# Another order for two early steps of a fused attention and feed-forward kernel: states ahead of outputs, first rows by token blocks, a copy split over two engines

## The chip, the cores and the metric

The kernel runs on one core of one Trainium2 chip. The metric is the device time of one execution in microseconds (us). Before the change it was 206.26 us, the median of three runs (206.10 to 206.67). TensorE is the matmul engine; VectorE, ScalarE and GpSimd are the three engines for elementwise work (DVE, ACT and POOL in the profile); SyncE issues the transfers.

## The reference

A linear attention with a decay per head (4 batches, 8 heads, 768 positions, head size 64) feeds a feed-forward layer with 512 inputs, 2048 hidden units and a tanh gelu. All inputs and the output are 32-bit floats.

```python
for b in range(nb):                       # 12 blocks of 64 positions
    intra = einsum('bhic,bhjc->bhij', qb, kb) * Dmask
    intra = einsum('bhij,bhjd->bhid', intra, vb)
    inter = einsum('bhid,bhde->bhie', qb * lam_pow, kv_state)
    out[:, :, sl] = intra + inter
    kv_state = lam_block * kv_state + einsum('bhsd,bhse->bhde', kb * rev_pow, vb)
# ... (x = out as 3072 tokens of 512 numbers)
h = x @ w_in                              # 512 -> 2048
return gelu_tanh(h) @ w_out               # 2048 -> 512
```

## The kernel before

The attention is worked through in 24 steps (12 blocks of 256 positions, each for two halves of the heads). A step is: scale q, k and v (`prep`), transpose q and k on TensorE and copy them back (`stage_t`), form the scores, mask them (`causal`), form the products with v for the state and for the outputs (`products`), copy x out (`x_out`), and update the state (`update`, part "t" on VectorE, part "u" on GpSimd). Two PSUM banks, `OK`, hold the state products (columns 256 and up) and the outputs (columns 0 to 255) of one step.

The feed-forward part waits in a list of small pieces, `filler`; `fill(n)` draws the next n pieces into TensorE's program between the attention's steps. Weights arrive as 32-bit floats and are cast. Here is the stretch that the change rewrites, as code, with cuts marked. The first rows of the feed-forward part (`Hps`) need x of steps 0 and 1 for token block 0 and x of steps 2 and 3 for token block 1, and chunks c = 0, 1 or 2, 3 of w_in.

```python
def x_out(s, OK):                                   # x of one step, two banks
    ...
    for c in range(2):
        pin(nc.scalar.activation(out=dst[...], in_=OK[c][:, 0:256]..., func=AF.Copy))

# first rows of group 0: (chunks, token blocks, last)
((0, 1), both, False), ((2, 3), b0, False), ((2, 3), b1, True)
...
update(1, 0)
idle(3)                        # three products that nobody reads
scores(2); products(2, None)
causal(2); prep_v(3)
update(2, 0); update(1, 1); update(2, 1, "t")
idle(2)
stage_t(3)
OK1 = products(None, 1, evacuate=False)[0]
OK2 = products(None, 2, evacuate=False)[0]
x_out(2, OK2); x_out(1, OK1)
scores(3)
banks = products(3, None)
update(3, 0)
cast_win(0, 0, 256, 128, c01)                       # VectorE, two casts
cast_win(0, 256, 512, 256, c01, on_act=True)
causal(3); queue_group(0)
fill(4)
products(None, 3, banks)
cast_win(0, 0, 512, 256, c23)
fill(8)
...
cast_wout(1, (POOL, ACT)); cast_wout(3, (POOL, ACT))
fill(9)                                             # output sums O2, four products each
prep(4); stage_t(4)                                 # q of step 4 on VectorE, then the transposes
```

The transposes of step 4 stand in TensorE's program behind nine pieces of the output sums and need q of step 4 from VectorE. And the results of the output sums go out through three buffers, so the fourth one of group 0 needs the first to have left:

```python
o32 = otp.tile([P, DM], FP32, tag="o32", name="o32")          # otp has 3 buffers
pin(nc.scalar.activation(out=o32[:], in_=O2.pop(tau)[0][:], func=AF.Copy))
pin(nc.sync.dma_start(out=out[...], in_=o32[:]))
```

Of the kernel before, what the change touches and what calls it, by code (L numbers as in the profile page):

```python
# [10 lines left out]
AF = mybir.ActivationFunctionType  # L11
# [4 lines left out]
def kernel(  # L16
# [217 lines left out]
    def stage_t(s):  # L234
        if s >= FIRST_DMA_T:
            return
        tq, tk = a16[s][:2]
        Tps = ps_M.tile([P, 2, 2, 2, P], FP16, tag="M", name="Tps")
        for i, t in enumerate((tq, tk)):
            for hp in range(2):  # L240
                for j in range(2):
                    pin(nc.tensor.transpose(Tps[:, i, j, hp, :], t[:, j, 2 * hp : 2 * hp + 2, :],  # L242
                                            ident[:]))
        o = qkp.tile([P, 2, 2, 2, P], FP16, tag="qkT", name=f"qkT_{s}")
        if s == 2:
            pin(nc.scalar.activation(out=o[:, 0], in_=Tps[:, 0], func=AF.Copy))
            pin(nc.vector.tensor_copy(out=o[:, 1], in_=Tps[:, 1]))
        elif s in (1, 3, 5, 6):
            pin(nc.scalar.activation(out=o[:], in_=Tps[:], func=AF.Copy))
        else:  # L250
            pin(nc.vector.tensor_copy(out=o[:], in_=Tps[:]))
        qkT[s] = o
# [33 lines left out]
    def products(n, s, banks=None, evacuate=True):  # L286


        OK, opened = banks or ([ps_M.tile([P, 512], FP32, tag="M", name=f"OK{c}")
                                for c in range(2)], set())  # L290

        def start(c, hl):
            if (c, hl) in opened:
                return False
            opened.add((c, hl))
            return True

        if n is not None:
            _, tk, tv = a16[n]
            last = (n // 2) % NSB == NSB - 1  # L300
            for jk in range(2):
                for hp in range(2):
                    for c, hl in TILES:
                        if c == 1 and last:
                            continue
                        pin(nc.tensor.matmul(  # L306
                            OK[c][half64(hl), 256 + hp * D : 256 + hp * D + D],
                            tk[half64(c), jk, 2 * hp + hl, :], tv[half64(c), jk, 2 * hp + hl, :],
                            start=start(c, hl), stop=(jk == 1), skip_group_check=True))
            Kps[n] = OK  # L310
        if s is None:
            return OK, opened
        sbg, half = divmod(s, 2)
        o = qkT.pop(s)
        PT = PTs.pop(s)
        _, _, tv = a16.pop(s)
        for hp in range(2):
            for jk in range(2):
                for c, hl in TILES:
                    pin(nc.tensor.matmul(  # L320
                        OK[c][half64(hl), hp * P : hp * P + P], tv[half64(c), jk, 2 * hp + hl, :],
                        PT[half64(c), hl, hp, jk, :], start=start(c, hl), stop=False,
                        skip_group_check=True))
        for c in range(2):
            if c == 0 and sbg % NSB == 0:
                continue
            u = us.pop((s, 0) if c else (s - 2, 1))
            for hp in range(2):
                pin(nc.tensor.matmul(OK[c][:, hp * P : hp * P + P], u[:, hp].rearrange("p l d -> p (l d)"),  # L329
                                     o[:, 0, :, hp, half64(c)], start=False, stop=True,  # L330
                                     skip_group_check=True))
        if evacuate:
            x_out(s, OK)
        return OK, opened

    def x_out(s, OK):
        sbg, half = divmod(s, 2)
        g, i = group_of[sbg]
        if g not in xT:
            xT[g] = xtp.tile([P, 2, len(groups[g]), 2, SB], FP16, tag="xT", name=f"xT_{g}")  # L340
        dst = xT[g][:, half, i]
        for c in range(2):
            pin(nc.scalar.activation(  # L343
                out=dst[:, :, c * P : (c + 1) * P].rearrange("p hp (t j) -> p hp j t", j=2),
                in_=OK[c][:, 0:256].rearrange("p (hp j t) -> p hp j t", hp=2, j=2),
                func=AF.Copy))

    us = {}

    def update(s, c, parts="tu"):  # L350


        sbg, half = divmod(s, 2)
        sb = sbg % NSB
        if c == 1 and sb == NSB - 1:
            Kps.pop(s)
            return
        if "t" in parts:
            OK = Kps[s] if c == 0 else Kps.pop(s)
            K = OK[c][:, 256:384].rearrange("p (hp d) -> p hp d", hp=2)  # L360
            t = ucp.tile([P, 2, D], FP32, tag=f"t{half}", name=f"t_{s}_{c}")
            if sb == 0 and c == 0:
                pin(nc.vector.tensor_copy(out=t[:], in_=K))
            else:
                for hp in range(2):
                    pin(nc.vector.scalar_tensor_tensor(  # L366
                        t[:, hp, :], state[half][:, hp, :],
                        lamu[:, 2 * half + hp : 2 * half + hp + 1], K[:, hp, :],
                        ALU.mult, ALU.add))
            state[half] = t  # L370
        if "u" in parts:
            u = ubp.tile([P, 2, 2, D], FP16, tag=f"u{half}", name=f"u_{s}_{c}")
            pin(nc.gpsimd.tensor_tensor(  # L373
                u[:], state[half][:].unsqueeze(2).to_broadcast([P, 2, 2, D]),
                lumask[:, 2 * half : 2 * half + 2, :].unsqueeze(3).to_broadcast([P, 2, 2, D]),
                ALU.mult))
            us[(s, c)] = u
# [6 lines left out]
    def queue_group(g):  # L384
# [124 lines left out]

        def mm1_part(f, cs, blocks, last):  # L510

            if cs[0] == 0:
                first[f] = ps_M.tile([P, N], FP32, tag="M", name="Hps")
            for c in cs:
                pin(nc.tensor.matmul(by_block(first[f][:])[:, blocks],  # L515
                                     w_in16[:, c, f * P : (f + 1) * P], x(c)[:, blocks],
                                     start=(c == 0), stop=last and c == NC - 1,
                                     skip_group_check=True))
            if last:
                pin(nc.scalar.activation(out=gT[:, f % HF, f // HF, :], in_=first.pop(f)[:],  # L520
                                         func=AF.Gelu_apprx_tanh))

        if g == 0:
            both, b0, b1 = slice(0, 2), slice(0, 1), slice(1, 2)
            for fs, stages in ((range(4), (((0, 1), both, False), ((2, 3), b0, False),
                                           ((2, 3), b1, True))),
                               (range(4, 8), (((0, 1), both, False), ((2, 3), both, True)))):
                for stage in stages:
                    for f in fs:
                        filler.append(lambda f=f, stage=stage: mm1_part(f, *stage))  # L530
            for f in range(8, NF):
                filler.append(lambda f=f: mm1([f]))
            order = [(tau, part) for part in (0, 2, 1, 3) for tau in range(3)]
            order += [(3, part) for part in (0, 2, 1, 3)]
            for tau, part in order:
                filler.append(lambda tau=tau, part=part: mm2(tau, part))
            return
# [35 lines left out]
    def idle(n):  # L573

        t = ps_M.tile([P, 512], FP32, tag="M", name="idle")
        for _ in range(n):
            pin(nc.tensor.matmul(t[:], ones[:, 0:P], ones[:], start=True, stop=True))
# [40 lines left out]
    stage_t(2)  # L618
    prep_qk(3)
    update(1, 0)  # L620
    idle(3)
    scores(2)
    products(2, None)
    causal(2)
    prep_v(3)
    update(2, 0)
    update(1, 1)
    update(2, 1, "t")
    idle(2)
    stage_t(3)  # L630
    OK1 = products(None, 1, evacuate=False)[0]
    OK2 = products(None, 2, evacuate=False)[0]
    x_out(2, OK2)
    x_out(1, OK1)
    scores(3)
    banks = products(3, None)
    update(3, 0)
    c01, c23 = slice(0, 2), slice(2, 4)
    cast_win(0, 0, 256, 128, c01)
    cast_win(0, 256, 512, 256, c01, on_act=True)  # L640
    causal(3)
    queue_group(0)
    fill(4)
    products(None, 3, banks)
    cast_win(0, 0, 512, 256, c23)
    fill(8)
    cast_win(1, 0, 512, 256, c01)
    update(3, 1, "t")
    cast_win(1, 0, 512, 256, c23)
    fill(8)  # L650
    update(2, 1, "u")
# [83 lines left out]
```

## Time and profile before

| | before |
|---|---|
| time, median of 3 runs (lowest, highest) | 206.26 us (206.10, 206.67) |
| span of the profiled run | 204.3 us |
| TensorE busy | 196.8 us, 96% |
| TensorE busy from 20 to 180 us | 159.94 of 160 us |
| first feed-forward product / idle just before it | 18.08 us / 0.77 us |
| granted TensorE clock, 10 to 180 us | 1.00 |

How to read a row of a timeline: start, duration, engine, source line, operation, what is written and read, how many instructions the row joins, and in square brackets the idle time of the engine just before the row and what ended it. A row without brackets began with no idle time of note. Line numbers of the changed kernel are two or three higher than before (L401 becomes L403, L515 becomes L518, L366 becomes L368), because the change adds lines above; the copy of x, L343, becomes L348 on ScalarE and L346 on VectorE.

The kernel is bound by TensorE with no idle time from 20 us to its tail. So the only idle time to win lies ahead of 20 us, and whether a gain there reaches the end depends on whether TensorE later meets something that it doesn't set itself. The rows that show this are in the prediction.

### The profile page before, as it was taken

How to read it: one execution, taken by the hardware profiler on the slowest of the kernel's cores; microseconds unless marked ns; L12 is line 12 of the kernel's file. 1: busy time of each engine (PE TensorE's matmuls, PEld its weight loads, DVE VectorE, ACT ScalarE, POOL GpSimd, SP SyncE). 2: the span in 40 equal slices, each digit the busy share in tenths (PEclk: the TensorE clock that was granted, in tenths of full speed). 3: DMA queues.
4: the chain of work that ended last, by engine and by line, in shares of the span. 5: the costliest groups of instructions: out<-in, count | busy, mean ns of one | idle time of the engine just before them, and what ended most of it. 6: DMA issues, size and time to landing. Idle time of an engine off the chain costs nothing.

```text
span 204.3 us, 5584 instructions
## 1 busy us (share of the span) xinstructions
PE 196.8 (96%) x2321; PEld 127.6 (62%) x2321; DVE 144.8 (71%) x271; ACT 107.7 (53%) x204; POOL 70.1 (34%) x80
## 2 busy tenths in 40 slices
PE   7888999999999999999999999999999999999992
PEld 2454644456875788654688654788554788545881
DVE  4887627867599999929997828996739673136552
ACT  2364678475683573477722477641576331577110
POOL 5595123646487750436134404314412100000000
PEclk9999999999999999999999999999999999999999
DMA  4999999999999999996449993647330003300014
GB/s 132 299 321 385 387 388 379 285 291 315 297 262 228 296 241 173 235 285 176 91 128 266 181 279 94 152 107 156 75 85 0 0 3 103 107 0 0 3 51 156
DMA packets 64074, 37.86 MB, mean 185 GB/s; under 512 B 17712, under 2 KB 59184, under 8 KB 64048
## 3 DMA queue, kind: packets, MB, share of 16 engines
q1 hardware_dynamic: 63760, 37.24, 68.1%
q8 instruction: 18, 0.29, 0.6%
q10 hardware_dynamic: 288, 0.26, 0.4%
q14 instruction: 8, 0.07, 0.1%
HBM read 27.27 MB, written 6.29 MB: 164 GB/s over the span
## 4 chain that ended last, share of the span: by engine, by line
PE 89%; DMA 3%; SPq 2%; ACT 1%; DVE 1%; issue 1%
PE Hps L401 37%; PE O2ps L416 10%; PE MB L470 8%; PE MA L470 7%; PE MD L470 7%; PE Sps L271 4%; PE MC L470 4%; PE Hps L515 4%; PE OK L329 3%; PE OK L320 3%; DMA k<-in_k_dram 3%; SPq L68 2%; PE OK L306 1%; PE Tps L242 1%; DVE t L366 1%
## 5 line engine op out<-in xcount | busy, mean ns | idle before, releaser
L401 PE MATMUL Hps<-xT,w_in 128*128 128x512 f16 (+1 forms) x416 | 79.1, 346 | 0.0
L405 ACT ACTIVATE gT<-Hps 128x512 f16<-128x512 f32 x88 | 52.1, 598 | 21.9 <-PE Hps L401 21.1
L401 PEld LDWEIGHTS <-w_in 128*128 128x128 f16 x416 | 40.2, 98 | 33.5
L373 POOL TENSOR_TENSOR u<-t,lumask 128x256 f16<-128x256 f32 x40 | 31.4, 792 | 80.6 <-DVE t L366 58.4
L446 DVE TENSOR_TENSOR gs<-gT 128x512 f16<-128x512 f16 (+1 forms) x70 | 36.6, 586 | 10.8 <-ACT gT L405 10.6
L280 DVE TENSOR_TENSOR PT<-Sps,mask 128x1024 f16<-128x1024 f32 x24 | 29.2, 1216 | 17.1 <-PE Sps L271 17.1
L470 PEld LDWEIGHTS <-gs 128*128 128x128 f16 x360 | 34.9, 98 | 4.0
L211 POOL TENSOR_TENSOR v<-v,dv 128x512 f16<-128x512 f32 x24 | 29.2, 1220 | 4.9 <-DMA v<-in_v_dram 4.8
L343 ACT ACTIVATE xT<-OK 128x256 f16<-128x256 f32 x48 | 18.2, 454 | 20.0 <-PE OK L329 14.3
L416 PE MATMUL O2ps<-w_out,gT 128*128 128x512 f16 x96 | 21.9, 379 | 0.0
L226 ACT ACTIVATE qk<-k 128x512 f16<-128x512 f32 x24 | 15.0, 626 | 9.3 <-DMA k<-in_k_dram 9.3
L221 DVE TENSOR_TENSOR qk<-q,dq 128x512 f16<-128x512 f32 x23 | 19.3, 841 | 0.0
L477 ACT ACTIVATE m<-MB 128x512 f32<-128x512 f32 x9 | 5.4, 597 | 25.4 <-PE MB L470 25.4
L470 PE MATMUL MA<-w_sum,gT 128*128 128x256 f16 x144 | 17.5, 273 | 0.1
L470 PE MATMUL MD<-w_sum,gs 128*128 128x256 f16 x136 | 17.5, 273 | 0.0
L470 PE MATMUL MB<-w_out,gs 128*128 128x256 f16 x144 | 17.2, 273 | 0.0
L366 DVE SCALAR_TENSOR_TENSOR t<-t,lamu,OK 128x64 f32<-128x64 f32 x64 | 14.5, 273 | 2.3 <-PE OK L306 1.1
L470 PEld LDWEIGHTS <-gT 128*128 128x128 f16 x144 | 14.0, 98 | 2.8 <-ACT gT L405 0.3
L416 PEld LDWEIGHTS <-gT 128*128 128x128 f16 x96 | 9.2, 98 | 9.9
L481 DVE TENSOR_TENSOR o<-MA,m 128x512 f32<-128x512 f32 x9 | 6.2, 688 | 12.3 <-ACT m L477 12.3
L271 PEld LDWEIGHTS <-qkT 64*64 64x64 f16 x384 | 6.2, 106 | 8.6 <-issue 4.2
L123 DVE TENSOR_TENSOR w_sum<-wo,wo 128x1024 f16<-128x1024 f32 x6 | 7.9, 1362 | 4.2 <-DMA wo<-in_moe_w_out_dram 4.2
(55 smaller groups left out, 168.8 us busy)
## 6 DMA issues: line engine op xcount, KB each, us to landing
q<-in_q_dram SPq DMA_DIRECT2D x24, 256.0 KB, 4.5
k<-in_k_dram SPq DMA_DIRECT2D x24, 256.0 KB, 4.9
v<-in_v_dram SPq DMA_DIRECT2D x24, 256.0 KB, 4.9
out_dram<-o SPq DMA_DIRECT2D x22, 256.0 KB, 4.1
wo<-in_moe_w_out_dram SPq DMA_DIRECT2D x4, 1024.0 KB, 9.2
wi<-in_moe_w_in_dram SPq DMA_DIRECT2D x4, 512.0 KB, 8.0
wi<-in_moe_w_in_dram SPq DMA_DIRECT2D x2, 1024.0 KB, 12.5
out_dram<-o SPq DMA_DIRECT2D x2, 128.0 KB, 1.9
```

Source lines behind the costliest of these rows:

```text
L211: pin(nc.gpsimd.tensor_tensor(wide(tv[:]), ld32[s][2][:], decay(dv, s), ALU.mult))
L221: pin(q_eng.tensor_tensor(wide(tq), q32[:], decay(dq, s), ALU.mult))
L226: pin(nc.scalar.activation(out=wide(tk), in_=k32[:], func=AF.Copy))
L280: pin(nc.vector.tensor_tensor(t[:].rearrange("p a b c d -> p (a b) (c d)"), Ss.pop(n)[:].rearrange("p a b c d -> p (a b) (c d)"), mask[:]. ...
L343: pin(nc.scalar.activation(out=dst[:, :, c * P : (c + 1) * P].rearrange("p hp (t j) -> p hp j t", j=2), in_=OK[c][:, 0:256].rearrange("p ( ...
L366: pin(nc.vector.scalar_tensor_tensor(t[:, hp, :], state[half][:, hp, :], lamu[:, 2 * half + hp : 2 * half + hp + 1], K[:, hp, :], ALU.mult ...
L373: pin(nc.gpsimd.tensor_tensor(u[:], state[half][:].unsqueeze(2).to_broadcast([P, 2, 2, D]), lumask[:, 2 * half : 2 * half + 2, :].unsqueez ...
L401: pin(nc.tensor.matmul(by_block(Hps[:, i, :]), w_in16[:, c, f * P : (f + 1) * P], x(c), start=(c == 0), stop=(c == NC - 1)))
L405: pin(nc.scalar.activation(out=dst, in_=Hps[:], func=AF.Gelu_apprx_tanh))
L416: pin(nc.tensor.matmul(O2[tau][0][:], gT[:, f % HF, f // HF, tau * P : (tau + 1) * P], w_out16[:, f, :], start=(n == 0), stop=(n == NF - 1)))
L446: pin(nc.vector.tensor_tensor(gsum[m][:, i, :], block(T0, F0, i), block(T1, F1, i), op))
L470: pin(nc.tensor.matmul(dst, lhsT, rhs, start=(i == 0), stop=(i == HF - 1), skip_group_check=True))
```

## The change

The intent is to let TensorE reach its unbroken stretch earlier. The states of steps 1 and 2 go ahead of the mask of step 2; two unread products go; the transposed q and k of step 3 are copied by two engines; the first casts of w_in come ahead of the state of step 3; the first rows are drawn by token blocks, so that the first of them need neither x of step 2 nor of step 3, and four more of them stand ahead of step 3's outputs; x of step 3 is copied out by ScalarE and VectorE together. The diff, with the plain plumbing of the token blocks cut:

```diff
@@ stage_t
-        if s == 2:
+        if s in (2, 3):
             pin(nc.scalar.activation(out=o[:, 0], in_=Tps[:, 0], func=AF.Copy))
             pin(nc.vector.tensor_copy(out=o[:, 1], in_=Tps[:, 1]))
-        elif s in (1, 3, 5, 6):
+        elif s in (1, 5, 6):
             pin(nc.scalar.activation(out=o[:], in_=Tps[:], func=AF.Copy))
@@ x_out
-    def x_out(s, OK):
+    def x_out(s, OK, second=None):
...
+            if c == 1 and second is not None:
+                pin(second.tensor_copy(out=d, in_=o))
+            else:
+                pin(nc.scalar.activation(out=d, in_=o, func=AF.Copy))
@@ first rows of group 0
-            for fs, stages in ((range(4), (((0, 1), both, False), ((2, 3), b0, False),
-                                           ((2, 3), b1, True))),
+            for fs, stages in ((range(4), (((0, 1), b0, False), ((0, 1), b1, False),
+                                           ((2, 3), b0, False), ((2, 3), b1, True))),
@@ steps 2 and 3
     update(1, 0)
+    update(1, 1, "t")
     idle(3)
     scores(2)
     products(2, None)
+    update(2, 0)
     causal(2)
     prep_v(3)
-    update(2, 0)
-    update(1, 1)
+    update(1, 1, "u")
+    stage_t(3)
+    products(None, 1)
+    products(None, 2)
     update(2, 1, "t")
-    idle(2)
-    stage_t(3)
-    OK1 = products(None, 1, evacuate=False)[0]
-    OK2 = products(None, 2, evacuate=False)[0]
-    x_out(2, OK2)
-    x_out(1, OK1)
     scores(3)
     banks = products(3, None)
-    update(3, 0)
     c01, c23 = slice(0, 2), slice(2, 4)
     cast_win(0, 0, 256, 128, c01)
     cast_win(0, 256, 512, 256, c01, on_act=True)
+    update(3, 0)
     causal(3)
     queue_group(0)
-    fill(4)
-    products(None, 3, banks)
-    cast_win(0, 0, 512, 256, c23)
     fill(8)
+    cast_win(0, 0, 256, 256, c23, on_act=True)
+    cast_win(0, 256, 512, 256, c23)
+    fill(2)
+    products(None, 3, banks, evacuate=False)
+    x_out(3, banks[0], nc.vector)
+    fill(6)
+    update(3, 1, "t")
     cast_win(1, 0, 512, 256, c01)
-    update(3, 1, "t")
     cast_win(1, 0, 512, 256, c23)
     fill(8)
```

More of the change, by code (lines that the diff above doesn't have):

```diff
@@ L342, in x_out @@
         for c in range(2):
-            pin(nc.scalar.activation(
-                out=dst[:, :, c * P : (c + 1) * P].rearrange("p hp (t j) -> p hp j t", j=2),
-                in_=OK[c][:, 0:256].rearrange("p (hp j t) -> p hp j t", hp=2, j=2),
-                func=AF.Copy))
+            d = dst[:, :, c * P : (c + 1) * P].rearrange("p hp (t j) -> p hp j t", j=2)
+            o = OK[c][:, 0:256].rearrange("p (hp j t) -> p hp j t", hp=2, j=2)
+            if c == 1 and second is not None:
+                pin(second.tensor_copy(out=d, in_=o))
+            else:
+                pin(nc.scalar.activation(out=d, in_=o, func=AF.Copy))
     us = {}
@@ L510, in mm1_part @@
         def mm1_part(f, cs, blocks, last):
-            if cs[0] == 0:
+            opens = f not in first
+            if opens:
                 first[f] = ps_M.tile([P, N], FP32, tag="M", name="Hps")
@@ L516, in mm1_part @@
                                      w_in16[:, c, f * P : (f + 1) * P], x(c)[:, blocks],
-                                     start=(c == 0), stop=last and c == NC - 1,
+                                     start=opens and c == 0, stop=last and c == NC - 1,
                                      skip_group_check=True))
```

## The prediction

> **What bounds the kernel now.** I read the page first, for which engine fills the span; then the chain of waits, for what that engine waits for; then the timelines of 9 to 27 us, the only place where it waits.
>
> ```profile
> PE 196.8 (96%) x2321; PEld 127.6 (62%) x2321; DVE 144.8 (71%) x271; ACT 107.7 (53%) x204; POOL 70.1 (34%) x80
> PE   7888999999999999999999999999999999999992
> PE 89%; DMA 3%; SPq 2%; ACT 1%; DVE 1%; issue 1%
> ```
>
> TensorE is busy for 96% of 204.3 us and makes 89% of the chain. The tenths show where it is not full: the first four slices (20 us) and the tail. In the table by stretches it is busy for 3.99 of the 5 us from 15 to 20 us, and for 159.9 of the 160 us from 20 to 180 us at full granted clock. So the change, which only touches steps 2 and 3 and the first rows of the feed-forward part, can at best make TensorE reach its unbroken stretch earlier. From the timeline of TensorE:
>
> ```profile
> 13.41 0.42 PE L271 MATMUL Sps<-qkT 64*64 64x128 f16 x16 [0.50 <-DVE qkT L247]
> 15.92 0.41 PE L320 MATMUL OK<-PT,v 64*64 64x128 f16 x15 [0.17 <-DVE t L366]
> 18.08 2.11 PE L515 MATMUL Hps<-xT,w_in 128*128 128x512 f16 x8 [0.77 <-DVE w_in L107]
> ```
>
> The number in brackets is idle time before the row, with its releaser. The last row is the start of the first rows: TensorE waits 0.77 us for the first cast of w_in. VectorE's timeline says why the cast is late, and that it is slow:
>
> ```profile
> 15.02 1.23 DVE L366 SCALAR_TENSOR_TENSOR t<-t,lamu,OK 128x64 f32<-128x64 f32 x6
> 17.35 0.47 DVE L366 SCALAR_TENSOR_TENSOR t<-t,lamu,OK 128x64 f32<-128x64 f32 x2 [1.10 <-PE OK L306]
> 17.74 0.93 DVE L107 CAST w_in<-wi 128x256 f16<-128x256 f32 x2
> 17.90 1.24 POOL L373 TENSOR_TENSOR u<-t,lumask 128x256 f16<-128x256 f32 x2 [0.99 <-DVE t L366]
> ```
>
> VectorE stands idle for 1.10 us until the products of step 3 come, updates the state, and only then casts. One cast alone is 0.285 us (the shortest of its group); the two took 0.93 together, and the second ends at 18.67, just after GpSimd's first u (18.5).
>
> [...]0.93 us for two casts beside two u, and 1.52 us instead of 0.69 for the q product at 38.69 us beside a w_out cast on GpSimd. [...]the granted clock is 1.00 in all stretches[...].
>
> **The change part by part,** with the compiled order of both kernels and durations of the trace before.
>
> *States ahead of causal(2).* Both states of step 1 and 2 (four 0.19 us steps) go ahead of causal(2), which moves from 13.88 to about 14.4 and ends at 15.6. The products of step 2 then start at 15.6 instead of 15.92 (they no longer wait for the state that releases their bank): 0.3 us.
>
> *Removed unread products.* Two, 0.43 us of TensorE. The transposes behind them wait for q of step 3 (GpSimd, 14.05) anyhow: worth nothing by itself.
>
> *qkT of step 3 halved.* 0.60 on ScalarE, then 0.42 on VectorE behind causal(2): ready at about 15.95 instead of 16.0. Scores and products of step 3 come some 0.3 us earlier.
>
> *Casts ahead of the state of step 3.* The first half of w_in's first block was issued at 10.10 and landed 7.1 us later, at 17.2. So the first cast runs at 17.22 to 17.51 and TensorE starts at about 17.55 instead of 18.08: 0.5 us, and no more, since the transfer is the limit. GpSimd has no u then, so the second cast ends at 17.8 and not at 18.67.
>
> *First rows by blocks.* Eight 128x512 products (0.216 us each: 1.73) become sixteen of 128x256 (0.109: 1.75): no cost. Four of 128x256 are drawn ahead of the outputs of step 3. TensorE then does its sixteen to 19.35, four to 19.8 (the ScalarE cast of the second half, landed at 18.57, ends at 19.25), the outputs of step 3 to 20.45, where before they ended at 20.87. It is then ahead by 0.42 plus the four products (0.43): **0.85 us**.
>
> *x of step 3 on two engines.* Both outputs end by about 20.95, when TensorE has done four more products; before, ScalarE ended at 21.56. Behind it the casts of the next block are tight: GpSimd's u of step 3 lands on the second one, which may cost 0.25 us.
>
> **Where the 0.85 us goes.** TensorE has no more idle time, so an early start would come out whole if nothing else that it needs had a time of its own. But transfers do: the mean DMA share stays between 0.97 and 1.08 in every stretch from 15 to 54 us (stretches of 1 to 5 us), and no load in there waits for TensorE. I therefore looked for what is near its need already.
>
> First, transposes of step 4: TensorE begins them at 40.61; q of step 4 is ready at 38.69+1.52 = 40.21, behind the w_out casts, which follow their transfers. Ahead by 0.85, TensorE would wait until about 40.27, and keep **0.34 us**.
>
> Second, ScalarE at 53 us:
>
> ```profile
> 52.97 0.60 ACT L422 ACTIVATE o<-O2ps 128x512 f32<-128x512 f32 x1 [2.36 <-DMA out_dram<-o]
> 53.98 1.56 ACT L405 ACTIVATE gT<-Hps 128x512 f16<-128x512 f32 x3
> 54.48 0.28 PE L329 MATMUL OK<-qkT,u 128*128 128x128 f16 x2
> 54.62 1.58 PE L401 MATMUL Hps<-xT,w_in 128*128 128x256 f16 x13
> ```
>
> ScalarE stands for 2.36 us until the first output tile (issued 46.13, landing 6.7 us later) has left its buffer; there are three, and this is the fourth tile. Behind it in ScalarE's queue stand k of step 8 and the first gelu of the second group, 53.98 to 54.58. In the compiled order the Hps product at 54.62 waits for exactly this gelu, which frees its bank. TensorE came there with at most 0.02 us to spare: after the two L329 rows at 59.35 the next product follows in 0.12 us, here in 0.14. So already now this spot is set by TensorE and the output transfer at once. A TensorE that comes earlier waits there, and keeps nearly **nothing**. Behind it all goes as before.
>
> Sum: 0.85 gained, 0.5 lost at 40 us, 0.34 at 54.6 us. What remains is that the two clocks vary from run to run: I give it 0.1 to 0.15 us. 206.26 - 0.15 = **206.1 us**.
>
> **Rivals.**
> A. *The gain survives whole.* If transfers came earlier too, or the output tile's landing had slack, 0.85 us would stay: 205.4. For it: TensorE at 99.9% from 20 to 180 us. Against it: the DMA share of about 1 since 15 us, and the output's issue at 46.13 stands directly behind loads in one queue, without a wait for ScalarE (its tile was ready at 43.0).
> B. *Only the wait at 40 us counts:* 0.34 us, 205.9. It needs the landing near 52.8 us to move by 0.3, which the little freedom of the queue might do by chance.
> C. *The start itself fails.* The second cast of the next block behind GpSimd, or qkT of step 3 behind causal(2), takes the place of the removed waits. Then 0.3 to 0.5 of the 0.85 us goes already at 16 to 22 us; the time stays at 206.2.
> D. *Slower.* VectorE takes a half of qkT and of x, about 0.8 us more, in a window where it is busy for 3.9 of 5 us. A state that comes late would cost 0.3 us at most: 206.5.
>
> **Range and chances.** A at 205.4 and D at 206.5 bound it, and the three runs of before spread by 0.57 us: 205.4 to 206.5. Two per cent is 4.1 us, and the whole idle time of TensorE up to 20 us is 3.7 us (10 less 7.86, 5 less 4.47, 5 less 3.99): within 2% is nearly certain.
>
> **What would show it.** Right: the first Hps product at about 17.55 behind a cast that waits for the transfer of w_in; outputs of step 3 done by 20.5; an idle row of 0.2 to 0.5 us ahead of the transposes near 40.3 us; the fourth output tile on ScalarE still near 53.0; a wait of 0.2 to 0.4 us ahead of the Hps product near 54.6; and equal times of the same rows from 55 us on. Wrong: no wait there and rows from 60 us on earlier by more than 0.3 us (A or B), or a first Hps product not before 17.9 us (C).

## The result, and the profile after

| | before | after |
|---|---|---|
| time, median (lowest, highest; runs) | 206.44 us (206.10, 206.67; 4) | 205.81 us (205.76, 205.93; 4) |
| ratio after / before, 95% interval | | 0.9972 (0.9954 to 0.9989) |
| time of the profiled run | 206.10 us | 205.82 us |
| span of the profiled run | 204.3 us | 204.0 us |

A ratio is the mean time of one kernel's fast runs over that of the other's of the same rounds, so it is not quite the ratio of the quoted medians. The change is worth 0.2 to 0.3%: within 2%, as predicted, and inside the range of times expected. Note that the two profiled runs differ by 0.28 us and the medians by 0.63 us, since the profiled run of the kernel before is its fastest. Rows of traces explain the 0.28 only.

The page of the changed kernel, its busy times and the chain that ended last, answering to those of before:

```profile
PE 196.4 (96%) x2327; PEld 128.0 (63%) x2327; DVE 145.0 (71%) x272; ACT 108.2 (53%) x204; POOL 69.6 (34%) x80
PE 88%; SPq 4%; DMA 3%; issue 1%; DVE 1%; ACT 1%
```

Nothing moved at this scale: TensorE is busy for 96% again, and the 40 slices of its row show the same digits as before. TensorE's timeline of the changed kernel, in the stretches that the prediction named:

```profile
14.36 0.74 PE L242 MATMUL Tps<-ident,qk 128*128 128x128 f16 x8 [0.19 <-POOL qk L221]
...
17.65 2.36 PE L518 MATMUL Hps<-xT,w_in 128*128 128x256 f16 x20 [0.55 <-DVE w_in L107]
20.52 5.20 PE L518 MATMUL Hps<-xT,w_in 128*128 128x256 f16 x28
25.56 1.67 PE L403 MATMUL Hps<-xT,w_in 128*128 128x512 f16 x7
...
32.47 7.93 PE L418 MATMUL O2ps<-w_out,gT 128*128 128x512 f16 x36
40.33 0.62 PE L242 MATMUL Tps<-ident,qk 128*128 128x128 f16 x8
...
54.33 1.91 PE L403 MATMUL Hps<-xT,w_in 128*128 128x256 f16 x16
...
199.20 1.04 PE L472 MATMUL ME<-w_sum,gs 128*128 128x256 f16 x8
```

And the same rows of TensorE's timeline of the kernel before that the prediction doesn't show:

```profile
20.71 5.39 PE L515 MATMUL Hps<-xT,w_in 128*128 128x256 f16 x32
25.93 1.24 PE L401 MATMUL Hps<-xT,w_in 128*128 128x512 f16 x5
...
32.84 7.93 PE L416 MATMUL O2ps<-w_out,gT 128*128 128x512 f16 x36
40.61 0.61 PE L242 MATMUL Tps<-ident,qk 128*128 128x128 f16 x8
...
199.49 1.04 PE L470 MATMUL ME<-w_sum,gs 128*128 128x256 f16 x8
```

Subtract row by row to follow the lead. At the first `Hps` product it is 18.08 - 17.65 = 0.43 us. Behind the outputs of step 3 it is 20.71 - 20.52 = 0.19 us plus four products already done (four of 0.109 us, 0.43), so 0.62 us. At 25.56 it is 0.37 us, at the output sums (32.47) 0.37, at the transposes of step 4 (40.33) 0.28, and at the last group of products (199.20) 0.29. So 0.25 us is lost between 20.5 and 25.6 us, 0.09 us at 40 us, and nothing in the 159 us after that.

The first loss has no bracket in TensorE's own rows, because rows are joined. It stands in the timeline of the weight loads (PEld) of the changed kernel:

```profile
20.47 0.37 PEld L518 LDWEIGHTS <-w_in 128*128 128x128 f16 x4
21.22 4.01 PEld L518 LDWEIGHTS <-w_in 128*128 128x128 f16 x24 [0.38 <-DVE xT L346]
```

Four weight loads follow the outputs of step 3, and the fifth waits for x of step 3. VectorE's timeline of the changed kernel says when that was written:

```profile
17.30 0.50 DVE L107 CAST w_in<-wi 128x256 f16<-128x256 f32 x2 [0.73 <-DMA wi<-in_moe_w_in_dram]
...
20.72 0.45 DVE L346 CAST xT<-OK 128x256 f16<-128x256 f32 x1 [1.00 <-PE OK L329]
```

The two first casts take 0.50 us and wait for the transfer of w_in, as the prediction said. The copy of x ends at 20.72 + 0.45 = 21.17, some 0.65 us after TensorE had started on the products behind the outputs (20.52). The four products that don't need it last 0.44 us. TensorE is then without work from 20.52 + 0.44 = 20.96 to about 21.22: 0.26 us. The row of 28 products confirms it. It joins twelve products of 128x256 and sixteen of 128x512 (only the first shape is printed), 12 x 0.109 + 16 x 0.216 = 4.76 us, and took 25.56 - 20.52 = 5.04 us. In the kernel before the row of 32 is sixteen of each shape, 5.20 us, and took 25.93 - 20.71 = 5.22.

The second loss is at the transposes of step 4. VectorE's timeline of the changed kernel has q of step 4, which they read, and the timeline of the weight loads has the wait:

```profile
38.76 1.52 DVE L221 TENSOR_TENSOR qk<-q,dq 128x512 f16<-128x512 f32 x1
```

```profile
40.33 0.45 PEld L242 LDWEIGHTS <-qk 128*128 128x128 f16 x8 [0.42 <-DVE qk L221]
```

It ends at 40.28, and the transposes begin at 40.33, at once behind it. The 36 products ahead of them took 7.77 us in the kernel before (40.61 - 32.84), so TensorE was done with them at 32.47 + 7.77 = 40.24 and stood for 0.09 us. In the kernel before q ended at 40.21, the weight loads had no such wait, and the transposes began at 40.61, because TensorE came no sooner. ScalarE at 53 us, which was to take the rest, in the changed kernel:

```profile
51.58 0.60 ACT L424 ACTIVATE o<-O2ps 128x512 f32<-128x512 f32 x1 [1.24 <-DMA out_dram<-o]
```

It still waits for the first output tile to leave, but the tile comes 1.39 us earlier than before (51.58 against 52.97). The view of the line that issues this transfer gives the reason. First the kernel before, then the changed one, both issued at 46.1 us:

```profile
DMA to landing us min/median/max: 6.6/6.7/6.7
```

```profile
DMA to landing us min/median/max: 5.2/5.3/5.3
```

### The profile page after: what moved, and what is told of

It is laid out like the page before. It is cut to its first block, busy times and chain, and to the rows that moved or that the text cites. A ratio compares the mean times of both kernels' runs of the same rounds, so it can differ in the third digit from the quotient of the medians.

```text
span 204.0 us, 5595 instructions
## 1 busy us (share of the span) xinstructions
PE 196.4 (96%) x2327; PEld 128.0 (63%) x2327; DVE 145.0 (71%) x272; ACT 108.2 (53%) x204; POOL 69.6 (34%) x80
## 4 chain that ended last, share of the span: by engine, by line
PE 88%; SPq 4%; DMA 3%; issue 1%; DVE 1%; ACT 1%
PE Hps L403 37%; PE O2ps L418 10%; PE MB L472 8%; PE MA L472 7%; PE MD L472 7%; SPq L68 4%; PE MC L472 4%; DMA wi<-in_moe_w_in_dram 3%; PE Sps L271 3%; PE Hps L518 3%; PE OK L329 3%; PE OK L320 3%; PE Tps L242 1%; PE OK L306 1%; PE ME L472 0%
## 5 line engine op out<-in xcount | busy, mean ns | idle before, releaser
L123 DVE TENSOR_TENSOR w_sum<-wo,wo 128x1024 f16<-128x1024 f32 x6 | 7.9, 1362 | 4.2 <-DMA wo<-in_moe_w_out_dram 4.2
```

## The experiments

All kernels gave correct results. Each was timed in five rounds beside the kernel before on the same chip. The first four ran on one chip (the kernel before: median 206.33 us, 205.84 to 206.65, 11 runs), the others on a second one (median 206.26, 205.89 to 207.53, 12 runs, the last four of the table sharing eleven of these with the four ahead of them). Two of the second chip's runs of the kernel before are late (207.53 and 207.48 us) and raise its mean by 0.2 us (0.1%), so the ratios there are to be read beside the medians. The column "Tps 4" is the start of the transposes of step 4 in the profiled run, "last" that of the last group of products.

| run | what it is | median us (lowest, highest) | ratio to before, 95% | Tps 4 | last | last - Tps 4 |
|---|---|---|---|---|---|---|
| before (first trace) | | 206.44 (206.10, 206.67) | | 40.61 | 199.49 | 158.88 |
| after (first trace) | the change | 205.81 (205.76, 205.93) | 0.9972 (0.9954, 0.9989) | 40.33 | 199.20 | 158.87 |
| before_again | before, repeated | 206.35 (206.11, 206.42) | 1.0005 (0.9993, 1.0017) | 40.65 | 199.50 | 158.85 |
| before_o4 | before, a fourth output place | 206.16 (205.91, 207.03) | 1.0006 (0.9987, 1.0026) | 40.67 | 199.53 | 158.86 |
| after_o4 | after, a fourth output place | 205.95 (205.89, 206.53) | 0.9994 (0.9980, 1.0008) | 40.45 | 199.32 | 158.87 |
| after_late_u | after, u of step 3 later | 206.36 (205.91, 207.74) | 0.9998 (0.9983, 1.0013) | 42.25 | 201.12 | 158.87 |
| after_again | after, repeated | 205.89 (205.73, 206.11) | 0.9979 (0.9958, 0.9999) | 40.51 | 199.38 | 158.87 |
| before_casts | before, only the casts moved | 205.88 (205.72, 206.05) | 0.9978 (0.9955, 1.0000) | 40.37 | 199.23 | 158.86 |
| after_t4h | after, two products ahead of Tps 4 | 205.91 (205.68, 206.00) | 0.9977 (0.9956, 0.9997) | 40.64 | 199.07 | 158.43 |
| after_t4hu | that, and u later | 205.82 (205.66, 206.47) | 0.9980 (0.9958, 1.0002) | 40.73 | 199.16 | 158.43 |
| after_x8 | after, x of step 3 covered | 205.75 (205.65, 205.89) | 0.9972 (0.9949, 0.9994) | 40.40 | 199.27 | 158.87 |
| after_x8_t4h | both | 205.68 (205.37, 207.09) | 0.9981 (0.9951, 1.0011) | 41.41 | 199.84 | 158.43 |
| after_x8_t4h_o4 | both, and a fourth output place | 205.51 (205.41, 205.70) | 0.9961 (0.9941, 0.9982) | 40.32 | 198.75 | 158.43 |
| after_idle2 | after, unread products back | 205.87 (205.75, 206.63) | 0.9983 (0.9960, 1.0006) | 40.27 | 199.12 | 158.85 |

The last column is the main finding. From the transposes of step 4 to the last products it is 158.85 to 158.88 us in every kernel with the old program order there, and 158.43 in every kernel that does two products (0.43 us) ahead of them. No traced run lost or gained more than 0.03 us from there to the last products, not even where the output tile landed early or late. So the time of a traced run is set by when TensorE gets to the transposes of step 4, and only losses up to there need explaining.

### Theory and rivals after the result

Theory: the lead is cut twice in series, by x of step 3 near 21 us and by q of step 4 at 40.3 us, and the wait that I had predicted at 54.6 us doesn't exist in ordinary runs. Rival 1: the output tile at 53 us does hold TensorE and the two landings in the traces, 6.7 and 5.3 us, are the difference. Rival 2: the casts of w_in's second block take longer beside GpSimd's u (four took 1.84 us in the changed kernel), and that is what is lost near 21 us.

### before_again

The kernel before, unchanged, to see what its first trace owed to chance.

> The kernel before, unchanged, for a second trace and for the spread of its time. In the first trace (a run of 206.1 us) the first output tile was issued at 46.13 and landed 6.7 us later; ScalarE could only take the fourth output tile at 52.97, and the Hps product at 54.62 then had 0.02 us to spare. Theory 'output gate': the runs near 206.65 are those in which this landing comes still later, so a trace of a slow run shows idle time of TensorE of about 0.5 us ahead of the Hps product near 54.6, and a landing 7 us or more after the issue. Rival 'start': the slow runs lose their half microsecond in the first 20 us, where TensorE waits for loads; then the first Hps product comes 0.3 to 0.5 us later than 18.08 and the gate at 54.6 shows no wait. Both expect a median between 206.1 and 206.7 and a ratio of 1.000.

Measured: 206.35 us, ratio 1.0005. The first product, the output sums and the transposes stand within 0.04 us of the first trace (18.12, 32.88, 40.65), but ScalarE's timeline has the fourth output tile 1.47 us earlier:

```profile
51.50 0.60 ACT L422 ACTIVATE o<-O2ps 128x512 f32<-128x512 f32 x1 [0.86 <-DMA out_dram<-o]
```

The tile landed 5.2 us after its issue instead of 6.7. So the landing that I had read as a fixed clock varies, and the first trace had the latest one of all fourteen (4.7 to 6.7).

### before_o4 and after_o4

The fourth output tile of group 0 goes to a staging tile that is free by then, so that it waits for no landing, in the kernel before and in the changed one alike:

```diff
-            o32 = otp.tile([P, DM], FP32, tag="o32", name="o32")
+            if g == 0 and tau == 3:
+                o32 = wst.tile([P, DM], FP32, tag="w32", name="o32w")
+            else:
+                o32 = otp.tile([P, DM], FP32, tag="o32", name="o32")
```

> The kernel before with a fourth output buffer for the first group (one of the weight staging tiles that are free by then), so that ScalarE's fourth output tile no longer waits for a transfer. Theory 'output gate': the slow runs disappear, the median falls to about 206.1, the spread to 0.2 us, 0.3 us below the kernel before. Rival 'start': no change, ratio within 0.0005 of 1, the spread stays at half a microsecond.

> The changed kernel with the same fourth output buffer. In its trace the landing came 5.3 us after the issue, so the gate had about 1.1 us to spare. If the gate is open in the changed kernel in most runs: same as the changed kernel, 205.8 us, ratio to before 0.997. If the gate costs the changed kernel something in the average (my prediction said that it takes all the rest of the gain), it is faster than 205.8 by up to 0.3 us.

Measured: 206.16 and 205.95 us, ratios 1.0006 and 0.9994, both intervals around 1. In the kernel before, the feed-forward product behind the scores near 54 us, the one in question, starts at 54.66 without the gate, and at 54.62 and 54.64 with it. From the transposes of step 4 to that product it is 13.99 to 14.01 us in all of them, with and without the gate, and 14.00 in the changed kernel. Rival 1 is out for these runs: even the landing of 6.7 us cost at most 0.02 us. Whether it would have held a TensorE that came 0.3 us earlier in just that run is not shown. The theory that this landing makes the slow runs is out too: without the gate the kernel before still spread from 205.91 to 207.03 us.

The ratio of after_o4 doesn't show the gain of the change: its median is 0.38 us below that of the kernel before, yet the ratio of means is 0.9994, in part because one run of 206.53 weighs in it. Single runs half a microsecond or more above the rest occur in many of the kernels.

### after_late_u

GpSimd's u of step 3 is put behind two casts of w_out, so that it can't stand beside VectorE's casts of w_in:

```diff
     update(2, 1, "u")
-    update(3, 1, "u")
...
     cast_wout(0, (POOL, POOL))
+    update(3, 1, "u")
```

> The changed kernel with GpSimd's last u of step 3 put behind two casts of w_out[...]. Prediction's own step: the four casts take 1.42 us instead of 1.84, TensorE's rows to 25.3 instead of 25.56 us (0.28 us of waits gone), but the wait for q of step 4 at 40.3 us takes it all back: the transposes of step 4 start at 40.3 again and the time stays at 205.8 (within 0.1 us). Rival, that early starts come out whole: 205.5 us.

Measured: 206.36 us, ratio 0.9998, no gain, but the profiled run was an outlier of 207.74 us and says little of u. It says something else. VectorE's timeline has the next block of w_in 1.94 us later than in the changed kernel (24.01), and TensorE's timeline shows the wait for q of step 4:

```profile
25.95 1.29 DVE L107 CAST w_in<-wi 128x1024 f16<-128x1024 f32 x2 [2.46 <-DMA wi<-in_moe_w_in_dram]
```

```profile
42.25 0.62 PE L242 MATMUL Tps<-ident,qk 128*128 128x128 f16 x8 [0.70 <-DVE qk L221]
```

The transposes came 1.92 us later and the run took 1.92 us longer (207.74 - 205.82). In this run, with late transfers, q of step 4 ended 1.91 us later too (40.67 + 1.52 = 42.19, against 40.28), and the time followed it one for one. Its other five runs (205.91 to 206.63) are late on the whole too, which is not explained; the same later u in after_t4hu gave 205.82. As a test of u the run was inconclusive, so u was tried again below.

### after_again

> The changed kernel once more, on one chip with the three others, for its own spread and a second trace. Expected: about 0.3 us below the kernel before, as in the traces (the Hps product near 54.5 came 0.29 us earlier than in the trace before, the last product 0.29 us earlier). In the trace: transposes of step 4 start within 0.1 us of the end of VectorE's q product of step 4 (about 40.3 us), so that it sits on that wait; output landing between 4.7 and 6.7 us after the issue.

Measured: 205.89 us, ratio 0.9979. The change's gain holds on this second chip: 0.34 us between the medians (206.23 - 205.89), 0.2%. First product 17.58, behind the outputs 20.61, q of step 4 ready at 38.93 + 1.52 = 40.45, transposes at 40.51: again directly behind q.

### before_casts

One part alone in the kernel before: the casts of w_in's first block ahead of the state of step 3.

```diff
     banks = products(3, None)
-    update(3, 0)
     c01, c23 = slice(0, 2), slice(2, 4)
     cast_win(0, 0, 256, 128, c01)
     cast_win(0, 256, 512, 256, c01, on_act=True)
+    update(3, 0)
     causal(3)
```

> The kernel before with one part of the change alone: the first casts of w_in ahead of the state of step 3, nothing else. Theory 'wait for q of step 4 caps every gain': the first Hps product starts near 17.6 instead of 18.1, TensorE is ahead by 0.4 to 0.6 us at its first O2 product (32.3 instead of 32.85), but the transposes of step 4 start at 40.3 as in the changed kernel, and the time equals that of the changed kernel within 0.1 us (about 0.3 us below before). Rival, that all parts add: it is slower than the changed kernel by 0.2 us or more.

Measured: 205.88 us, ratio 0.9978: one moved line gives as much as the whole change, within the noise. TensorE's timeline:

```profile
17.83 2.12 PE L515 MATMUL Hps<-xT,w_in 128*128 128x512 f16 x8 [0.27 <-ACT xT L343]
20.46 5.39 PE L515 MATMUL Hps<-xT,w_in 128*128 128x256 f16 x32
...
40.37 0.61 PE L242 MATMUL Tps<-ident,qk 128*128 128x128 f16 x8
```

The first product now waits for x of step 2 and not for the cast, so it is later than in the changed kernel by 0.2 us; it leads the kernel before by 0.25. That lead stays whole to the row of the remaining hidden units (L401, 25.69, 0.24) and to 40.37 (0.24), since eight products stand behind the outputs of step 3 and TensorE doesn't outrun q of step 4, ready here at 40.10. The whole change had a lead of 0.62 us in its first trace and lost the surplus again. But the attention began later in this run: the scores of step 2 stand at 13.83 us, against 13.41 in the first trace of the kernel before. What the moved line alone gives at an equal beginning is not shown. The expected lead of 0.4 to 0.6 us and the wait for q did not come here.

### after_t4h and after_t4hu

Half a piece of the output sums, two products, is drawn ahead of the transposes of step 4:

```diff
+                if (tau, part) == (0, 3):
+                    filler.append(lambda: mm2(0, 3, 0, 2))
+                    filler.append(lambda: mm2(0, 3, 2, 4))
+                    continue
                 filler.append(lambda tau=tau, part=part: mm2(tau, part))
...
-    fill(9)
+    fill(10)
     prep(4)
     stage_t(4)
```

> The changed kernel with two O2 products (0.43 us) drawn from behind to ahead of the transposes of step 4, so that TensorE doesn't reach them before VectorE has q. Nothing else moves. Theory 'cap': the wait ahead of the transposes vanishes and TensorE keeps what it had at 32.5 us (0.37 us ahead of before in the first traces, against 0.28 behind the cap): about 0.1 us faster than the changed kernel, in the trace if not in the times. Rival 'no cap': no difference at all.

> The same with the late u too: both of the losses that the changed kernel has behind its start are taken away. Theory: casts of the second block of w_in 1.42 instead of 1.84 us, O2 products start near 32.2, no wait at 40, the last product about 0.35 us earlier than in the changed kernel: 0.6 us below before. If the output tile's landing at 52 to 53 us binds (it had 1.1 us to spare in the trace of the changed kernel, so 0.7 here), less. Rival: transfers move the time and nothing is gained over the changed kernel.

Measured: 205.91 and 205.82 us, not to be told from the changed kernel's 205.89 (0.1 us and about 0.35 us less had been expected). TensorE's timeline of after_t4h:

```profile
32.44 8.37 PE L418 MATMUL O2ps<-w_out,gT 128*128 128x512 f16 x38
40.64 0.61 PE L242 MATMUL Tps<-ident,qk 128*128 128x128 f16 x8
```

38 products follow each other without a gap, (40.64 - 32.44)/38 = 0.216 us each, and q was there at 40.29. So the wait of 0.09 us is gone, and the last group starts at 199.07 instead of 199.20. There was no more to win at 40 us, because the stall near 21 us had already taken the rest of the lead.

after_t4hu adds the later u, this time in a run with ordinary transfers. VectorE's timeline, then that of the weight loads:

```profile
21.51 1.43 DVE L107 CAST w_in<-wi 128x512 f16<-128x512 f32 x4
```

```profile
21.28 2.71 PEld L518 LDWEIGHTS <-w_in 128*128 128x128 f16 x18 [0.38 <-DVE xT L346]
```

The four casts take 1.43 us. In the changed kernel, beside a u of 0.73 us on GpSimd (from 21.61), they took 1.84: one of them 836 ns, the other three 414 to 417. So u beside them cost VectorE 0.41 us. But TensorE's hole is the same, behind x of step 3 as before, and the 28 products take 25.62 - 20.58 = 5.04 us in both. Rival 2 is out: the loss beside u exists and isn't on TensorE's path.

### after_x8

All eight products of chunks 2 and 3 on token block 0, which need no x of step 3, stand behind its outputs. In the changed kernel four of them stood ahead:

```diff
     cast_win(0, 256, 512, 256, c23)
-    fill(2)
     products(None, 3, banks, evacuate=False)
     x_out(3, banks[0], nc.vector)
-    fill(6)
+    fill(8)
```

> In the changed kernel TensorE runs out of drawn products while x of step 3 is written (stall of about 0.27 us near 21.2 us). Here eight 128x256 products (0.87 us) instead of four stand behind the outputs of step 3, and two fewer stand ahead of them, so x (about 0.65 us after the outputs) is covered. Theory (the lead is lost again at the transposes of step 4, which wait for q from VectorE at about 40.3): the stall goes, the second expert block and the first O2 product start 0.2 to 0.3 earlier (25.3 and 32.2), but the transposes of step 4 still start at 40.3 to 40.5 and the time stays at the changed kernel's 205.85, within 0.1. Rival (the stall is what the gain lacks): 205.55 to 205.65.

Measured: 205.75 us, ratio 0.9972. TensorE's timeline:

```profile
20.14 5.36 PE L518 MATMUL Hps<-xT,w_in 128*128 128x256 f16 x32
25.34 1.89 PE L403 MATMUL Hps<-xT,w_in 128*128 128x512 f16 x8
...
32.24 7.93 PE L418 MATMUL O2ps<-w_out,gT 128*128 128x512 f16 x36
40.40 0.62 PE L242 MATMUL Tps<-ident,qk 128*128 128x128 f16 x8 [0.23 <-DVE qk L221]
```

The hole near 21 us is gone (no weight load waits for x), and the row of the remaining hidden units (25.34) and the output sums (32.24) start 0.22 and 0.23 us earlier than in the changed kernel. Then the transposes wait for q, visibly now: the 36 products need 7.77 us and the transposes come 8.16 us after their start, 0.39 us of waiting (the bracket shows 0.23, as the modelled end of the last product covers the rest). They start at 40.40, later than in the changed kernel by 0.07, since q is ready at 40.35 instead of 40.28. What the first loss gives back, the second takes. The median is 0.14 us below after_again's, with ranges that overlap: at the edge of what the theory expected (205.85 within 0.1) and 0.1 above the rival's 205.65, so here the trace decides and not the time.

### after_x8_t4h and after_x8_t4h_o4

Both edits together; and both with the fourth output place of above.

> Both losses taken away: eight products behind the outputs of step 3, and two products (0.43 us) of the O2 sums drawn ahead of the transposes of step 4, which then have q when they come. Theory (two losses in series, neither alone pays): the last product ends 0.35 to 0.5 earlier than in the changed kernel (198.7 to 198.85 instead of 199.2) and the time is about 205.5. Rival (the landing of the first output tile near 53 us holds TensorE once the lead is over about 0.4): the scores after the gelu start no earlier than 54.2 and the time stays at 205.8.

> As the run before, with a fourth place for output tiles, so that the output copy near 53 us never waits for a landing. Theory: same as the run before when the landing takes under 6 us, up to 0.2 us better when it takes longer: about 205.5. Rival (landing binds): 0.2 to 0.3 us better than the run before, 205.5 against 205.8.

Measured: 205.68 us with two late runs of the six (206.45 and 207.09; the other four are 205.37 to 205.75), and 205.51 us (205.41 to 205.70). The profiled run of the first is one of the late ones. Its TensorE timeline shows a third thing to wait for, the cast of w_out on GpSimd, that the two products moved forward read:

```profile
40.86 0.59 PE L418 MATMUL O2ps<-w_out,gT 128*128 128x512 f16 x2 [0.16 <-POOL w_out L117]
```

But q of step 4 was late in this run too (ready at 39.83 + 1.52 = 41.35), and the transposes, at 41.41, stand directly behind it again.

The second is the best version. Its TensorE timeline:

```profile
20.01 5.36 PE L521 MATMUL Hps<-xT,w_in 128*128 128x256 f16 x32
...
32.12 8.37 PE L418 MATMUL O2ps<-w_out,gT 128*128 128x512 f16 x38
40.32 0.61 PE L242 MATMUL Tps<-ident,qk 128*128 128x128 f16 x8
...
198.75 1.04 PE L475 MATMUL ME<-w_sum,gs 128*128 128x256 f16 x8
```

Against the first trace of the kernel before, the lead is 0.70 us behind the outputs of step 3 (20.71 - 20.01, 32 products to go in both), 0.72 at 25.21, 0.72 at 32.12, 0.72 at 40.32 (0.29 and the two products, 0.43), and 0.74 at the end. The whole lead survives, and the medians differ by 0.75 us (206.26 - 205.51), ratio 0.9961. All of its six runs lie below all six of after_again (205.73 and up). Neither edit alone showed this; together, with the fourth output place, they do. Whether that place adds anything is open: the rival that the landing binds expected 0.2 to 0.3 us from it. The four lower runs of after_x8_t4h have a median of 205.51 as well, but they were picked after the times were known, and none of them was traced.

### after_idle2

The two unread products are put back ahead of the transposes of step 3 (`idle(2)` ahead of `stage_t(3)`).

> The changed kernel with the two unread 128x512 products put back ahead of the transposes of step 3. Those transposes wait for q from GpSimd until about 14.3 us anyway, and two products take about 0.43 us of the idle time before it. Theory: no change, 205.85 within 0.1, the transposes still start at about 14.4 and the first product of the expert blocks at about 17.6. Rival (the unread products were what held the start): 0.2 to 0.4 us slower, 206.1 to 206.3.

Measured: 205.87 us, within 0.02 of after_again. TensorE's timeline:

```profile
14.82 0.61 PE L242 MATMUL Tps<-ident,qk 128*128 128x128 f16 x8
...
17.50 0.61 PE L518 MATMUL Hps<-xT,w_in 128*128 128x256 f16 x4
```

They stand at 14.38 to 14.82 and push the transposes back, which was not expected (these start 0.92 us behind the scores of step 2 at 13.90, against 0.73 in the changed kernel), and the first product doesn't mind: it comes at 17.50, when w_in is cast. The scores of step 3 stand 2.94 us behind those of step 2 with them and 2.93 without. Removing them is worth nothing by itself, as predicted, and the granted clock of the profiled run is 1.00 with them and, in the changed kernel's first trace, without.

## Why the prediction came out as it did

**What bounds the kernel: right.** The chain of work, the slices and the 159 us of constant length behind 40 us show one engine at work without a hole. What made the second loss hard to see is that a wait can be hidden by joined rows and modelled ends: the transposes at 40.33 have no bracket in TensorE's own timeline of the changed kernel. The timeline of the weight loads has one (0.42 us for q), and q ends at 40.28 in VectorE's.

**The start: right.** The first product came at 17.65 (17.48 to 17.70 in runs with ordinary transfers), against 17.55; the first cast waits for the transfer of w_in. Outputs of step 3 were done by about 20.5, as said. before_casts shows that the cast's place alone pays as much as the whole. The parts ahead of it did what they were to do: scores of step 3 come 2.93 to 2.94 us behind the scores of step 2 in all traces of changed kernels (16.56 - 13.63 in the first) and 3.18 to 3.21 in the four with the old order (16.62 - 13.41), about the 0.3 us forecast. In the first trace TensorE then waited for the cast all the same (0.55 us), so there it was only slack.

**The lead of 0.85 us: too large.** It was 0.62 us in the changed kernel behind the outputs of step 3, and 0.70 in the best version. Of the 0.23 us missing in the changed kernel, 0.10 is the first product (0.43 us earlier instead of 0.53) and 0.04 more lies ahead of the outputs (19.94 and not 19.80). The last 0.09 was never there: the prediction's sum took the outputs as 0.75 us long before (20.12 to 20.87, a row's modelled end) and as 0.65 us after (19.8 to 20.45). From start to start they save 20.12 - 19.80 = 0.32 and not 0.42 us.

**"Both outputs end by about 20.95, when TensorE has done four more products": the step that failed on the way.** The term was mis-sized. x of step 3 was ready at 21.07 on ScalarE and 21.17 on VectorE, 0.65 us behind the start of the four products, which last 0.44 us. It cost 0.26 us. The prediction put the risk there on the other wait, "GpSimd's u of step 3 lands on the second one, which may cost 0.25 us": u did land on it and cost VectorE 0.41 us, and TensorE nothing (after_t4hu).

**The transposes of step 4: the wait right, its size not.** They start directly behind q of step 4 in after, after_again and after_o4. In the first trace they lose 0.09 us, not 0.5, and the idle row of 0.2 to 0.5 us named as a sign didn't show, since less lead arrived there than I thought. (What stands ahead of q on VectorE are the sums of w_out, L123, and not its casts, as the prediction had it.) after_x8 shows that the wait takes up to 0.39 us when more lead arrives, and after_x8_t4h_o4 that two products ahead of it give it back.

**The wait at 54.6 us: wrong.** "A TensorE that comes earlier waits there, and keeps nearly nothing." I took the landing of one output tile, 6.7 us in one trace, for a fixed clock. In the other thirteen traces the same transfer took 4.7 to 6.3 us, and from the transposes of step 4 to that product it is 14.00 us with and without the gate. The wait never took anything in a run that was traced, and the rows behind it, said to come at equal times, come 0.29 us earlier. So rival B came closest: 0.29 us kept in the traces, and the landing was earlier, as B needed. But B had the whole loss at 40 us, and the traces have 0.25 of it near 21 us and 0.09 at 40.

**The time: within the range, 0.3 us below the centre.** The centre had 0.15 us left of the gain; the traces have 0.28 and the medians 0.34 (after_again) to 0.63, at ratios of 0.9979 and 0.9972. That it lies within the range says little: the range of 205.4 to 206.5 holds the unchanged time, 206.26, too. And it was in part luck, since a lead that was put 0.23 us too high stood against a loss at 54.6 us that never came. Why the medians differ by more than the traces is not settled. The traced runs of the kernel before (206.10, 206.11) and of before_o4 (206.17) are at its fast side, and none of its slower ordinary runs near 206.4 was traced. The traces offer a candidate. The scores of step 2, which the change doesn't move (2.83 us behind those of step 1 in the first trace before, 2.84 after), begin anywhere from 13.28 to 13.95 us in runs with ordinary transfers. In the kernel before and before_o4 the first feed-forward product stands 4.51 to 4.84 us behind them (18.08 - 13.41 = 4.67), and the first cast stands behind the state of step 3 (17.35 + 0.47, 17.74). In the changed kernels it stays at 17.48 to 17.70 (beginnings of 13.37 to 13.95), behind a cast that comes at 17.01 to 17.35 after waiting for the transfer. So a beginning at 13.9 us would put it at about 18.6 us in the kernel before, by estimate from these numbers. All three traces of that order began by 13.63 and had it at 18.08 to 18.14, so this is not shown.

## What to carry to other kernels

Where one engine is busy throughout, as TensorE is here (159.94 of 160 us before the change), a gain at the start is worth what the tightest later meeting with another clock leaves of it (0.28 of 0.62 us in the changed kernel's first trace). Two such meetings in series hid each other here: repairing either alone moved the median by at most 0.14 us, and repairing both by 0.38 us (205.89 - 205.51, with the fourth output place). Before calling a transfer's landing a clock that binds, look at it in a second run (4.7 to 6.7 us in fourteen traces here), and compare the length of the rest of the program between runs: if it is constant (158.85 to 158.88 us in ten runs here), nothing behind that point made the difference between these runs.
